# F of all chunks loaded four tokens a partition, its gate sums by 32-row tiles, and a new order

## The chip, the cores and the metric

The kernel runs on one core of a Trainium2 chip. The metric is the device time of one execution, in microseconds. Three runs of the kernel before took 181.86, 181.94 and 181.51 us, median 181.86.

## The reference

A gated linear attention (4 batches, 8 heads, 768 tokens, 48 columns a head) feeds a two-layer network without biases:

```python
f = 1.0 / (1.0 + np.exp(-f_logit))
for t in range(S):
    state = f[:, :, t, :, None] * state + np.einsum('bhd,bhe->bhde', k[:, :, t], v[:, :, t])
    y[:, :, t] = np.einsum('bhd,bhde->bhe', q[:, :, t], state)
x = y as [3072 tokens, 384]
h = x @ w_in                    # 384 x 2048
out = np.maximum(0.01 * h, h) @ w_out   # 2048 x 384
```

## The kernel before

**Tiling.** The 768 tokens are cut into 6 chunks of 128. A unit `u` is one chunk of one batch: 24 units, units 0 to 3 being the first chunk. For a unit, with `g` the running sum of log(1 + exp(-f_logit)) inside the chunk, K is scaled by exp(g) (`em`) and Q by exp(-g) (`a`); both are turned so that the head's columns lie on partitions; scores are their product, masked to the lower triangle (`mask`); `mix` adds the masked scores times V and Q times the state of the batch; `state` adds K times V to the state, which is then multiplied by the decay of the whole chunk (`a_end`). The 128 x 384 result `xn` of a unit is turned (`x`) and goes through the network: `up` makes 256 of the 2048 columns of `h` for a pair of units `m` (6 products of 256 columns), `up_act` takes them out of PSUM through the leaky ReLU, `down` makes one half (8 products of 384 columns) of a unit's output, and `put` and `out_dma` bring it out.

**The gate sums.** For units 4 to 23, `load_part(u, "f", ...)` loads F of one unit with a token on each partition, so every run of bytes is 48 numbers, 192 bytes, as it is for K, Q and V. ACT takes exp (`gate_exp`, L307) and ln (`gate_ln`, L310); `gate_pe` makes the running sums with one product against the triangle `ut` (L316) and the sums of the whole chunk with four one-column products (L319), all in one bank of PSUM; `decay_em` (L323), `decay_a` (L326) and a small exp (L328) take them out.

**The first chunk** has functions of its own, named `q_...`. Its F, K and Q are loaded four tokens a partition (runs of 768 bytes): batch `b` lies on every fourth partition from `b`. `q_gate_pe(hh, pp, bk)` makes the sums of one pair of heads for all four batches with four products of 512 columns (L226), `q_decay_act` (L230) takes them into `emT` and `aT` (which lie in the buffers `gT4` and `gT3`), `q_turn_pe` turns K and Q, and `q_mul` (L247) multiplies them on DVE, 256 columns at a time. `idle_pe` (L144) puts products of zeros into PE's queue where PE would otherwise stand still.

**The order.** One long list of calls, written out at the end of the kernel, gives every engine its order: each engine takes its instructions in the order of the list and waits for what they need. PSUM has eight banks, and every call names the bank that it uses. All loads of K, Q, V and F, the transposes by DMA and the stores go through SP's queue (at the start also ACT's); the weights W_in and W_out go through POOL's queue, cast to bf16 on the way (`load_w_in(0)` and `(1)` are the two halves of W_in). Outputs are stored from a pool of four buffers.

## Time and profile before

| | |
|---|---|
| runs | 181.51, 181.86, 181.94 us |
| span of the profiled execution | 181.4 us |
| what lies around the span | 0.5 us, taken as the median of the runs less the span |
| PE (matmul) busy | 172.7 us, 95% |
| weight loads, PE | 136.6 us, 75% |
| ACT busy | 121.5 us, 67% |
| DVE busy | 87.0 us, 48% |
| POOL busy | 55.7 us, 31% |
| DMA packets | 115014, of them 107440 under 512 bytes |
| read from HBM | 25.17 MB, written 4.72 MB |

The profile tells of one execution. PE is its matmul engine, PEld its weight loads, DVE the vector engine, ACT the scalar engine, POOL the GpSimd, SP the queue of most DMAs; a q behind a name (SPq) is an engine's sequencer. A busy PE is a bound from above, since the ends of its matmuls are modelled. A row of groups gives line, engine, operation, output and inputs, how often, the busy time, the mean of one in nanoseconds, and the idle time just before it with what ended it. The chain gives start, length and piece, in order of time.

### The profile page before, as it was taken

Reading aid. Unit: us, or ns where it says so; the run is one execution under the profiler, and the core shown is the slowest. Engines: PE = TensorE matmul, PEld = TensorE weight load, DVE = VectorE, ACT = ScalarE, POOL = GpSimd, SP = SyncE. Lnnn points to the kernel's source line nnn. Section 1 sums busy time; section 2 is a strip of 40 time slices with the busy share of each in tenths; the row PEclk is TensorE's granted clock in tenths of the full one; section 3 lists DMA queues with packets and bytes.
Section 4 is the critical chain, followed back from the end, with each engine's and each line's share of the span. In section 5 each row is a group of like instructions: output and inputs, shape, how many; then the busy total and the mean of one; then the engine's idle time right before and its main releaser. Section 6 shows DMA issues by size and latency. Waiting matters only on the chain.

```text
span 181.4 us, 4739 instructions
## 1 busy us (share of the span) xinstructions
PE 172.7 (95%) x1850; PEld 136.6 (75%) x1850; DVE 87.0 (48%) x193; ACT 121.5 (67%) x259; POOL 55.7 (31%) x109
## 2 busy tenths in 40 slices
PE   4999999999999999899999999999999999999993
PEld 2567799768679697697778677797786696796972
DVE  7449970253748538438465355374372370430000
ACT  2595789577979696496776777686763494471831
POOL 8092463122256532223415208313252220000000
PEclk9999999999999999999999999999999999999999
DMA  4999989989999999998999999999999796211202
GB/s 149 294 199 188 212 161 212 210 169 205 224 182 249 166 196 182 192 196 177 223 208 186 217 163 219 213 196 196 144 221 199 143 276 140 91 22 25 87 0 89
DMA packets 115014, 31.83 MB, mean 175 GB/s; under 512 B 107440, under 2 KB 113712, under 8 KB 114992
## 3 DMA queue, kind: packets, MB, share of 16 engines
q1 hardware_dynamic: 113072, 27.99, 80.8%
q0 software_dynamic: 1376, 3.15, 9.5%
q10 hardware_dynamic: 544, 0.39, 0.7%
q8 instruction: 14, 0.23, 0.6%
q14 instruction: 8, 0.07, 0.1%
HBM read 25.17 MB, written 4.72 MB: 165 GB/s over the span
## 4 chain that ended last, share of the span: by engine, by line
PE 61%; DMA 15%; SPq 12%; ACT 5%; issue 3%; DVE 1%; POOL 1%; ACTq 0%; POOLq 0%
PE ps L451 23%; PE ps L431 21%; DMA v_raw<-in_v_dram 6%; DMA f_raw<-in_f_logit_dram 6%; SPq L171 6%; SPq L347 5%; DMA fq<-in_f_logit_dram 3%; PE ps L226 2%; PE ps L442 2%; ACT gT L436 2%; PE ps L456 1%; PE ps L144 1%; SPq L475 1%; PE ps L390 1%; PE ps L398 1%
## 5 line engine op out<-in xcount | busy, mean ns | idle before, releaser
L451 PE MATMUL ps<-w_out_b,gT 128*128 128x384 bf16 x368 | 65.5, 326 | 0.0
L431 PE MATMUL ps<-xT,w_in 128*128 128x256 bf16 x528 | 64.4, 273 | 0.2 <-ACT gT L436 0.2
L436 ACT ACTIVATE gT<-ps 128x512 bf16<-128x512 f32 x88 | 51.4, 603 | 9.6 <-PE ps L431 7.7
L431 PEld LDWEIGHTS <-w_in 128*128 128x128 bf16 x528 | 55.9, 114 | 2.2 <-issue 0.4
L451 PEld LDWEIGHTS <-gT 128*128 128x128 bf16 x368 | 34.6, 98 | 19.8
L380 DVE TENSOR_TENSOR wm<-ps,ut 128x512 bf16<-128x512 f32 x40 | 25.2, 683 | 13.4 <-PE ps L369 12.6
L150 ACT COPY osb<-ps 128x384 f32<-128x384 f32 (+1 forms) x23 | 10.7, 465 | 17.8 <-PE ps L451 14.8
L300 POOL CAST sb<-sf 64x192 bf16<-64x192 f32 x40 | 14.3, 358 | 17.4 <-PE ps L387 11.6
L307 ACT ACTIVATE f_raw<-f_raw 128x384 f32<-128x384 f32 x20 | 10.6, 529 | 10.5 <-DMA f_raw<-in_f_logit_dram 10.3
L152 DVE CAST v_b<-v_raw 128x384 bf16<-128x384 f32 x15 | 7.9, 528 | 15.6 <-DMA v_raw<-in_v_dram 15.6
L335 POOL TENSOR_TENSOR kqh<-q_raw,a_t 128x384 bf16<-128x384 f32 x9 | 8.5, 945 | 20.4 <-ACT a_t L326 9.0
L331 POOL TENSOR_TENSOR kqh<-k_raw,em_t 128x384 bf16<-128x384 f32 x8 | 7.3, 916 | 22.7 <-ACT em_t L323 12.6
L323 ACT ACTIVATE em_t<-ps 128x384 bf16<-128x384 f32 x20 | 9.9, 494 | 4.8 <-PE ps L316 3.6
L331 DVE TENSOR_TENSOR kqh<-k_raw,em_t 128x384 bf16<-128x384 f32 x12 | 6.7, 556 | 10.4 <-ACT em_t L323 10.1
L412 POOL TENSOR_TENSOR sf<-sf,a_end 128x192 f32<-128x192 f32 x16 | 8.9, 556 | 7.1 <-DVE sf L407 6.7
L335 DVE TENSOR_TENSOR kqh<-q_raw,a_t 128x384 bf16<-128x384 f32 x11 | 7.5, 684 | 6.9 <-ACT a_t L326 6.7
L310 ACT ACTIVATE lf<-f_raw 128x384 bf16<-128x384 f32 x20 | 10.5, 527 | 0.3
L152 POOL CAST v_b<-v_raw 128x384 bf16<-128x384 f32 x9 | 4.7, 533 | 17.2 <-DMA v_raw<-in_v_dram 17.2
L326 ACT ACTIVATE a_t<-ps 128x384 bf16<-128x384 f32 x20 | 9.9, 495 | 0.0
L144 PE MATMUL ps<-fill 128*128 128x256 bf16 x47 | 8.5, 347 | 1.1 <-DVE uq L128 1.1
L406 DVE TENSOR_TENSOR sf<-sf,ps 64x192 f32<-64x192 f32 x16 | 5.5, 341 | 6.3 <-issue 3.5
L398 PE MATMUL ps<-v_b,kqh 128*128 128x96 bf16 x80 | 6.7, 206 | 1.2 <-DVE v_b L152 1.0
(88 smaller groups left out, 194.5 us busy)
## 6 DMA issues: line engine op xcount, KB each, us to landing
v_raw<-in_v_dram SPq DMA_DIRECT2D x24, 192.0 KB, 4.1
out_dram<-osb SPq DMA_DIRECT2D x23, 192.0 KB, 3.1
f_raw<-in_f_logit_dram SPq DMA_DIRECT2D x20, 192.0 KB, 4.0
k_raw<-in_k_dram SPq DMA_DIRECT2D x20, 192.0 KB, 4.3
q_raw<-in_q_dram SPq DMA_DIRECT2D x20, 192.0 KB, 4.2
w_in<-in_moe_w_in_dram POOLq DMA_DIRECT2D x2, 768.0 KB, 10.1
w_out_b<-in_moe_w_out_dram POOLq DMA_DIRECT2D x4, 384.0 KB, 7.1
kq<-in_k_dram SPq DMA_DIRECT2D x4, 192.0 KB, 4.5
```

Of the source, the lines that this page charges most:

```text
L150: eng.copy(out=out, in_=in_)
L152: eng.tensor_copy(out=out, in_=in_)
L171: nc.sync.dma_start(out=t, in_=src[b, :, c * C:(c + 1) * C, :].rearrange("h t d -> t h d"))
L300: nc.gpsimd.tensor_copy(out=state_b[b][r, :, e * D:(e + 1) * D], in_=state_f[b][r])
L307: nc.scalar.activation(raw[u]["f"], raw[u]["f"], AF.Exp, scale=-1.0)
L310: nc.scalar.activation(lfs[u % R_LF][:, :, 0:D], raw[u]["f"], AF.Ln, bias=1.0)
L331: eng.tensor_mul(khs[u % R_KQS][:, :, 0:D], raw[u]["k"], em_ts[u % R_EM])
L335: eng.tensor_mul(qhs[u % R_KQS][:, :, 0:D], r["q"], a_ts[u % R_EM])
L380: nc.vector.tensor_mul(wms[e][u % R_WM], bank(bk).rearrange("p (i n) -> p i n", i=P2), ut[:, None, :].to_broadcast([128, P2, 128]))
L431: nc.tensor.matmul(bank(bk)[:, i * 256:(i + 1) * 256], w_in_p[ff // 8][:, kk, ff // 4 % 2, :, ff % 4], xTs[m % R_XT][:, kk].rearrange("p a ...
L436: nc.scalar.activation(gTs[m % GBUFS][:, 2 * g:2 * g + 2].rearrange("p f a n -> p (f a n)"), bank(bk), AF.Prelu, alpha=0.01)
L451: nc.tensor.matmul(bank(bk)[:, 0:KD], g_part(u)[:, ff, :], w_out_b[:, ff, :], start=(ff == 0), stop=(ff == NF - 1))
```

## The change

- **F of chunks 1 to 5** is now loaded as that of the first chunk: `load_f(c, b)` puts the 128 tokens of batch `b` on the 32 partitions from 32 b, four tokens a partition (runs of 768 bytes). The four batches of a chunk fill one buffer: `fq` for even chunks, `kq` (after K of the first chunk) for odd ones. Exp and ln run for a whole chunk in two halves of 768 columns.
- **The running sums** of a chunk take 16 products (`gate_pe`, L330): for each of the four tokens a partition, one product for each batch, on the 32 partitions of that batch alone, into that batch's own bank. The matrix against which they run, `upto`, is made once by `upto_pe` and `put_upto`. The sums of the whole chunk take 16 products of four columns (`end_pe`) and one small exp (`end_act`), in place of four products and one small exp for each unit.
- **The first chunk:** the 32 partitions from 32 b hold batch `b` for F, K and Q, in place of every fourth partition. F comes in half loads (four heads), four on SP and four on ACT. The gate sums are made for a pair of batches and two pairs of heads in one bank; DVE's products `q_mul` take 512 columns.
- Outputs are stored from eight buffers, four of which lie in `qq`. The rings of raw loads have 7 buffers in place of 6.
- **The list of calls is new** as a whole.

Core of the diff:

```diff
-    R_RAW, R_KQS, R_LF, R_EM, R_AEND, R_V, R_KQT, R_WM, R_XN, R_XT = 6, 4, 3, 3, 8, 6, 4, 4, 4, 4
+    R_RAW, R_KQS, R_EM, R_V, R_KQT, R_WM, R_XN, R_XT = 7, 4, 8, 6, 4, 4, 4, 4
...
-        eng.dma_start(out=t[b::4, h, :, :].rearrange("p h j d -> p h (j d)"),
+        eng.dma_start(out=t[32 * b:32 * b + 32, h, :, :].rearrange("p h j d -> p h (j d)"),
...
-    first_load(nc.scalar, "f", 2)
-    first_load(nc.sync, "f", 0)
-    first_load(nc.sync, "f", 1)
-    first_load(nc.scalar, "f", 3)
...
+    for hh in range(2):
+        for b in range(B):
+            first_load((nc.sync, nc.scalar)[b // 2], "f", b, hh)
...
-    def q_gate_pe(hh, pp, bk):
-        for i in range(4):
-            nc.tensor.matmul(bank(bk), lfq[hh][:, i, 2 * pp:2 * pp + 2, :],
-                             steps[:, i].rearrange("p b t j -> p (b t j)"), start=(i == 0), stop=(i == 3))
+    def q_gate_pe(hh, bp, bk):
+        for pp in range(2):
+            for i in range(4):
+                nc.tensor.matmul(bank(bk)[:, 256 * pp:256 * pp + 256], lfq[hh][:, i, 2 * pp:2 * pp + 2, :],
+                                 steps[:, i, 2 * bp:2 * bp + 2].rearrange("p b j t -> p (b j t)"), start=(i == 0), stop=(i == 3))
...
+    def q_mul(dst, by, hh, bp, bk):
+        nc.vector.tensor_mul(dst[hh][:, bp].rearrange("p a b (t j) -> p (a b) j t", j=4),
+                             bank16(bk)[:, 512 * bp:512 * bp + 512].rearrange("p (m j t) -> p m j t", m=4, j=4),
+                             by[:, bp, 2 * hh:2 * hh + 2, :].rearrange("p a (b j t) -> p (a b) j t", b=2, j=4))
...
-        nc.tensor.matmul(cs[:, 0:H * D], ut, lf[:, :, 0:D], start=True, stop=True)
-        if c < NCH - 1:
-            for p in range(P2):
-                nc.tensor.matmul(cs[:, H * D + p:H * D + p + 1], lf[:, 2 * p:2 * p + 2, :], ones_col,
-                                 start=True, stop=True)
+    def load_f(c, b):
+        nc.sync.dma_start(out=fcs[c % 2][32 * b:32 * b + 32].rearrange("p h j d -> p h (j d)"),
+                          in_=f_logit[b, :, c * C:(c + 1) * C, :].rearrange("h (t j) d -> t h (j d)", j=4))
...
+    def upto_pe(bk):
+        for j in range(4):
+            nc.tensor.matmul(bank(bk)[:, j * 128:(j + 1) * 128], rows[:, j, :], ut, start=True, stop=True)
...
+    def gate_pe(c, *bks):
+        lf = lfc[c % 2]
+        for j in range(4):
+            for b in range(B):
+                r = slice(32 * b, 32 * b + 32)
+                nc.tensor.matmul(bank(bks[b])[:, 0:H * D], upto[r, j, :], lf[r, j, :, 0:D], start=(j == 0), stop=(j == 3))
+
+    def end_pe(c, bk):
+        for p in range(P2):
+            for j in range(4):
+                nc.tensor.matmul(bank(bk)[:, p * B:(p + 1) * B], lfc[c % 2][:, j, 2 * p:2 * p + 2, :], own,
+                                 start=(j == 0), stop=(j == 3))
...
     q_exp_act(0)
     q_ln_act(0)
-    load_part(0, "v", v)
     q_exp_act(1)
-    idle_pe(24, 7)
-    q_gate_pe(0, 1, 0)
+    idle_pe(24, 0)
+    idle_pe(19, 1)
+    q_gate_pe(0, 1, 2)
...
```

ACT at the start, first as it stood before, then as it stands now (`gT4` is `emT`, `gT3` is `aT`, `ps0` to `ps7` are the banks):

```order
L69 DMA fq_74<-in_f_logit_dram 32x8x192 x2
L82 ACT_TABLE_LOAD
L219 ACTIVATE fq_74<-fq_74 128x768
L222 ACTIVATE lfq0_117<-fq_74 128x16x48
L219 ACTIVATE fq_74<-fq_74 128x768
L222 ACTIVATE lfq1_118<-fq_74 128x16x48
L230 ACTIVATE gT4_236<-ps0_64 128x512
L230 ACTIVATE gT3_235<-ps0_64 128x512
L230 ACTIVATE gT3_235<-ps1_65 128x512
```

In the changed kernel ACT starts so:

```order
L76 ACT_TABLE_LOAD
L68 DMA fq_71<-in_f_logit_dram 32x4x192 x4
L212 ACTIVATE fq_71<-fq_71 128x768
...
L224 ACTIVATE gT4_237<-ps3_64 128x512
L224 ACTIVATE gT4_237<-ps4_65 128x512
L224 ACTIVATE gT4_237<-ps5_66 128x512
L224 ACTIVATE gT4_237<-ps2_63 128x512
L224 ACTIVATE gT3_236<-ps4_65 128x512
L145 CAST qhq0_121<-qq_73 128x16x48
L224 ACTIVATE gT3_236<-ps3_64 128x512
L224 ACTIVATE gT3_236<-ps5_66 128x512
L224 ACTIVATE gT3_236<-ps2_63 128x512
```

The table load moved ahead of the loads, the four decays of K stand ahead of those of Q, and one half of the cast of Q came to ACT, among the decays.

POOL at the end of its preparations, before and now:

```order
L183 COPY seen_237<-kq_75 128x1
L152 CAST khq0_119<-kq_75 128x16x48
L187 DMA w_in0_112<-in_moe_w_in_dram 128x3x1024
L187 DMA w_in1_113<-in_moe_w_in_dram 128x3x1024
L152 CAST qhq0_121<-qq_76 128x16x48
L152 CAST v_b0_206<-v_raw0_186 128x384
L152 CAST v_b1_207<-v_raw1_187 128x384
L268 TENSOR_TENSOR wm10_220<-wm10_220,ut_95 128x512
```

In the changed kernel the same place of POOL reads:

```order
L147 CAST qhq1_122<-qq_73 128x16x48
L180 DMA w_in1_113<-in_moe_w_in_dram 128x3x1024
L147 CAST v_b0_203<-v_raw0_178 128x384
L147 CAST v_b1_204<-v_raw1_179 128x384
L261 TENSOR_TENSOR wm10_217<-wm10_217,ut_96 128x512
L180 DMA w_in0_112<-in_moe_w_in_dram 128x3x1024
L261 TENSOR_TENSOR wm11_218<-wm11_218,ut_96 128x512
```

The two halves of W_in moved behind the cast of Q, the second of them also behind a mask of scores; the cast of K went to DVE.

PE at the first gate sums after the first chunk (unit 4 before, chunk 1 now):

```order
L316 LDWEIGHTS ut_95
L316 MATMUL ps7_71<-lf1_130,ut_95 128x384
L319 LDWEIGHTS lf1_130
L319 MATMUL ps7_71<-ones_col_110,lf1_130 128x1
...
L431 LDWEIGHTS w_in1_113
```

In the changed kernel PE has there, with each weight load after the first left out:

```order
L330 LDWEIGHTS upto_128
L330 MATMUL ps6_67<-lfc1_118,upto_128 128x384
...
L330 MATMUL ps1_62<-lfc1_118,upto_128 128x384
...
L330 MATMUL ps3_64<-lfc1_118,upto_128 128x384
...
L330 MATMUL ps5_66<-lfc1_118,upto_128 128x384
```

One product and four small ones into one bank became four rounds of these four products, into four banks in turn.

More of the change, by code (lines that the diff above doesn't have):

```diff
@@ new lines @@
+    turn_pe(4, 2)
+    down(3, 0, 6)
+    decay_em(7, 5)
+    decay_a(6, 3)
+    k_scale(V, 7)
+    turn_q(A, 4, 2)
+    put(A, 1, 7)
+    turn_k(V, 4, 2)
+    score1_pe(4, 5, 3)
+    load_f(2, 2)
+    k_scale(V, 6)
+    q_state_pool(2)
+    load_part(5, 'v', v)
+    decay_em(5, 1)
+    decay_a(5, 1)
+    q_scale(G, 6)
+    cast_v(A, 4)
+    end_pe(1, 7)
+    load_part(5, 'q', q)
+    mask(4, 0, 5)
+    end_act(1, 7)
+    put(A, 2, 4)
+    turn_pe(7, 2)
+    mask(4, 1, 3)
+    turn_q(A, 7, 2)
+    load_f(3, 2)
@@ new lines @@
+    x_pe(8, 2)
+    decay_a(12, 0)
+    down(6, 1, 3)
+    x_out(A, 8, 2)
+    mask(11, 1, 5)
+    decay_a(15, 7)
+    up(4, 3, 4)
+    load_f(4, 3)
+    mask(11, 0, 6)
+    out_dma(0)
+    mask(10, 1, 1)
+    cast_v(V, 10)
+    put(V, 6, 3)
+    up(4, 5, 2)
+    mix_pe(11, 5)
+    mix_pe(10, 6)
+    y_out(A, 10, 6)
+    load_part(15, 'v', v)
+    up(4, 4, 1)
+    y_out(A, 11, 5)
+    decay_em(12, 0)
+    up(4, 7, 3)
+    up(4, 6, 6)
+    decay_em(15, 7)
+    x_pe(10, 5)
+    x_pe(11, 0)
+    x_out(V, 11, 0)
@@ L1290 @@
+    out_dma(19)
+    up_act(11, 6, 7)
+    up(11, 3, 6)
+    up(11, 4, 3)
+    up_act(11, 3, 6)
+    up_act(11, 5, 1)
+    up_act(11, 4, 3)
+    up(11, 0, 7)
+    up_act(11, 0, 7)
+    down(20, 1, 5)
+    out_dma(18)
+    up_act(11, 2, 4)
+    put(A, 21, 0)
+    up_act(11, 7, 2)
+    down(22, 0, 6)
+    down(22, 1, 6)
+    out_dma(17)
+    down_cols(23, 192, 1)
+    put(V, 22, 6)
     out_dma(21)
[L1291 to L1294 removed]
+    out_dma(22)
+    put(V, 20, 5)
```

1650 lines of the change are left out of this document (771 added, 879 removed).

## Prediction

> **What bounds the kernel now.** I read the page first, then busy time by stretch, the groups inside the middle stretch, the chain of work that ended last, and the waits. The page's span, and two stretches (columns: length; busy us and count of PE, PEld, DVE, ACT, POOL; granted clock; DMA share; GB/s):
>
> ```profile
> span 181.4 us, 4739 instructions
> ```
>
> ```profile
> 21.20:54.00 32.80, 32.80 (x368) 26.44 (x366) 15.01 (x35) 25.43 (x55) 11.87 (x23) 1.00 0.99 195
> 54.00:132.00 78.00, 75.63 (x877) 61.68 (x875) 43.54 (x89) 58.00 (x133) 27.25 (x50) 1.00 1.12 196
> ```
>
> PE is the bound almost everywhere. From 21.2 on its visible idle time is 78.00 - 75.63 = 2.4 us, all of it in the second stretch, where the DMA share is 1.12. PE's ends are modelled, so I count that stretch as well: the largest and the smallest of its ten PE groups, and what one matmul costs in an unbroken run of the chain.
>
> ```profile
> L431 PE MATMUL ps<-xT,w_in 128*128 128x256 bf16 x275 | 34.2, 273 | 0.2 <-ACT gT L436 0.2
> L451 PE MATMUL ps<-w_out_b,gT 128*128 128x384 bf16 x156 | 28.6, 326 | 0.0
> ...
> L319 PE MATMUL ps<-ones_col,lf 128*128 128x1 bf16 x48 | 2.9, 164 | 0.0
> ```
>
> ```profile
> 34.70 0.45 PE ps L344 x8
> ...
> 81.71 0.55 PE ps L369 x16
> ...
> 141.07 0.16 PE ps L316
> ...
> 162.74 5.20 PE ps L451 x32
> 167.94 5.24 PE ps L431 x48
> ```
>
> A product of `up` costs 5.24/48 = 0.109 us, one of `down` 5.20/32 = 0.1625. So 275 x 0.109 + 156 x 0.1625 = 55.3, and the other eight groups by their own runs in the chain 18.1, together 73.4 us of work in 78. The waits are therefore between 2.4 us (visible) and 4.6 us (counted). What is late is mostly a load:
>
> ```profile
> POOL v_b L152 <- DMA v_raw<-in_v_dram: 17.2, 7, 5.7
> DVE v_b L152 <- DMA v_raw<-in_v_dram: 15.6, 14, 2.7
> ```
>
> The rest that isn't work is the start: the chain is 21.34 us old when the first `up` stands on it.
>
> ```profile
> 6.64 0.85 ACT fq L219
> 7.52 0.85 ACT lfq L222
> 8.41 1.90 PE ps L226 x8
> ...
> 13.83 1.42 PE ps L144 x13
> ...
> 21.34 2.62 PE ps L431 x24
> 23.96 0.23 PE ps L278 x8
> 24.20 0.17 PE ps L398 x4
> ```
>
> **The change, part by part.** The sum is made against the span, 181.4 us; the median of the runs, 181.86, is 0.46 above it.
>
> *The start until the first gate sum.* Before, 24 fill products stood ahead of it, behind a wait on `uq` (they share bank 7); now 43 stand there, on banks 0 and 1, with no such wait.
>
> ```profile
> 1.59 0.29 PE L124 MATMUL ps<-rep 128*128 128x128 bf16 x1 [1.59 <-POOL rep L93]
> 2.94 5.28 PE L144 MATMUL ps<-fill 128*128 128x256 bf16 x24 [1.06 <-DVE uq L128]
> ```
>
> They start at about 1.7. The 24 took 0.22 us each; later ones 1.42/13 = 0.109. With 24 slow and 19 fast that is 1.7 + 5.28 + 2.07 = 9.05, against 8.41 before. If the slow rate lasts until 8.4 by time rather than by count, 31 are slow and it is 9.8; if it ends by 5 us, 8.1. The half loads of F may land earlier, but the table load (1.28 us in before, then behind two loads) is now ahead of ACT's four; either way the fills cover it, so this earns nothing.
>
> *From there to the first `up`.* Three rows set the path, with the page's group rows for one instruction:
>
> ```profile
> L230 ACT ACTIVATE gT<-ps 128x512 f32<-128x512 f32 x8 | 4.0, 616 | 0.0
> L247 DVE TENSOR_TENSOR kTq<-ps,gT 128x256 bf16<-128x256 bf16 x8 | 3.0, 414 | 0.2 <-ACT gT L230 0.2
> L272 DVE TENSOR_TENSOR wm<-ps,ut 128x512 bf16<-128x512 f32 x6 | 3.8, 683 | 0.0
> ```
>
> The two gate sums end at 9.05 + 16 x 0.109 + 0.2 = 11.0. ACT then does four decays of K, one of Q, a cast of Q (0.85, as its other ops on 768 elements) and two more decays: 7 x 0.62 + 0.85 = 5.2, to 16.2. DVE's 512-column products have no row; the nearest, a mask of that size, gives 0.62 to 0.68, twice a 256-column one 0.83: I take 0.65. Eight then cost 5.2 instead of 16 x 0.414 = 6.6, but only the last three follow the late decays: 18.1. Six masks and a cast of V (at most another 7 x 0.62) reach 22.4, and the order puts `mix` and `state` of unit 3 (0.23 + 0.17, as in the chain at 23.96) ahead of the first `up`: 22.8, against 21.2. The same 0.4 us was done after the first `up` before, so the start costs +1.2 net; by the ends of the first step, +0.2 to +2.0.
>
> The order also puts the first half of W_in behind POOL's cast of Q, which waits for Q's landing, and past the cast of V; before, both halves went out ahead of it:
>
> ```profile
> 10.15 1.72 POOL L187 DMA_DIRECT2D w_in<-in_moe_w_in_dram x2
> 11.66 0.58 DVE L152 CAST qhq<-qq 128x768 bf16<-128x768 f32 x1 [2.27 <-DMA qq<-in_q_dram]
> 11.87 1.06 POOL L152 CAST qhq<-qq 128x768 bf16<-128x768 f32 x1
> DMA to landing us min/median/max: 8.3/10.1/11.9
> ```
>
> It goes out at 11.66 + 1.06 = 12.7 and lands at 21.0 to 24.6, median 22.8: just in time, 0 to +2 us. POOL's masks and V casts queue behind its 0.86 us, off the path. The second half follows a POOL mask at about 18.6 and lands at 26.9 to 30.5; its first reader is the eighth `up`, at 22.8 + 7 x 0.655 + 0.8 = 28.2. I take nothing for either.
>
> *The gate sums of the other five chunks.* Before, 4 x 0.16 = 0.64 us a chunk, and four one-column products a unit; now 16 products of 384 columns on 32 rows each, four neighbours on different rows and banks. No row shows 32 rows. One after the other they cost 16 x 0.163 = 2.6, four at once 0.65. The nearest row is that of 64 rows: 16 of 128 columns in 0.55 where full ones would take 2 x 0.45 = 0.90 (L344), 1.63 times of a possible 2. The same share of 4 is 3.27: 0.80, so +0.16 a chunk, +0.8 in all; ends 0 and +9.8. The column sums keep their count, 16 a chunk. The four products for `upto` add 0.2. The Trainium skill (TensorE: Matmul & The Clock Gate, Part 3) says that four row tiles of 32 rows run at once and measured 3.07 times; by it a chunk would cost 0.85 and the sum would be 0.25 us higher. The 64-row group agrees in kind; no row here shows 32 rows.
>
> The four sums hold four banks, and ACT needs 8 decays = 4.0 us to free them:
>
> ```profile
> L307 ACT ACTIVATE f_raw<-f_raw 128x384 f32<-128x384 f32 x20 | 10.6, 529 | 10.5 <-DMA f_raw<-in_f_logit_dram 10.3
> ...
> L323 ACT ACTIVATE em_t<-ps 128x384 bf16<-128x384 f32 x20 | 9.9, 494 | 4.8 <-PE ps L316 3.6 <-PE ps L319 0.8 <-issue 0.2
> ```
>
> Behind the sums of chunk 1, three halves of `down` (3 x 1.3) stand on PE, which need no ACT, so I cost it at nothing. Without that cover, a chunk would lose up to 4 us.
>
> *Exp and ln of F, the loads.* ACT has 40 instructions of 0.53 (L307 and its Ln) less and 20 of 0.85 more: 21.2 - 17.0 = 4.2 us less, and 12 small ones fewer. ACT is busy for 25.4 + 58.0 of the two stretches' 110.8 us, so this counts only through the waits. F's 20 loads keep their size but move runs of 768 bytes in place of 192. The two kinds of load side by side:
>
> ```profile
> 3.00:5.00 2.00, 2.00 (x10) 1.40 (x10) 2.00 (x8) 0.42 (x1) 1.68 (x5) 1.00 1.03 341
> 100.00:110.00 10.00, 9.55 (x100) 7.45 (x99) 4.23 (x10) 7.88 (x19) 2.70 (x5) 1.00 1.27 187
> ```
>
> The first window holds loads of the first chunk (768 bytes), the second mostly 192. A load of 196.6 KB takes 1.05 us of all queues at 187 GB/s and 0.58 at 341: 0.47 us a unit less, of 4.2 for a unit's four, where the DMA share was over 1. That can take all of the 2.4 to 4.6 us of waits, or nothing, if the new order puts its own in their place: POOL has 13 scalings of Q instead of 9, and all transposes, loads and stores still share SP's queue. I take -1.6, a third of the upper bound, because the new order gives V's loads other places in the queue too.
>
> **The sum:** +1.2 + 0.8 + 0.2 - 1.6 = +0.6: span 182.0, time 182.5 us. The tail, one DMA after the last columns, stays.
>
> **The rivals.**
> - *The loads were the whole trouble (faster).* All 4.6 us go and nothing takes their place: +1.2 + 1.0 - 4.6 = -2.4, time 179.5. For it: the waits above name loads, and every stretch of idle PE lies where the DMA share is over 1. Against: 21 to 54 has a share of 0.99 and no idle PE. It decides from 2.2 us of waits removed.
> - *New waits of the new order (slower).* Half of the new gate sums lose half of their cover, 5 x 0.5 x 2 = 5 us more: 187.5. It decides from 1 us on, as the forecast's gain from the waits is 1.6. For it: chunk 5's sums are followed by `up`, which needs ACT too. Against: banks alternate there with `down` between.
> - *Loads onto neighbouring partitions are slower (slower).* K and Q of the first chunk (8 x 0.197 MB, 4.6 us at 341 GB/s) now each fill 32 neighbours instead of every fourth partition. If that costs between nothing and half of the rate, Q lands 0 to 4.6 us later, 2.3 in the middle, and so does W_in's first half: 182.5 + 2.3 = 184.8. No row here shows neighbours. The Trainium skill (SBUF — State Buffer, Door 1: The DMA port swizzle) says that partitions 0 to 31 reach only 8 of 16 ports; by it the delay would be an estimated 2.6 us.
> - *The 32-row products run one after the other (the change doesn't do what it says).* +9.8 in place of +0.8: 191.5. Against: the 64-row row.
>
> **How the numbers follow.** Forecast 0.38 (182.5, its own range 181 to 184), faster rival 0.31, new waits 0.15, neighbours 0.10, one after the other 0.06. The range 178.6 to 187.8 leaves out the last and the outer ends. A difference of under 0.3% (181.3 to 182.4) can't be told from no change. Faster: the rival's 0.31 and 0.07 of the forecast's lower end, 0.38; within: 0.13 of the forecast's middle; slower: the other 0.18 of it and the last three, 0.49.
>
> **What would show it.** The first `up` at 22 to 23.5 with the first gate sum at 8.1 to 9.8; the gate group (32*128, 128x384) in runs of about 0.8 us for 16 in the chain; f loads landing in under 4.0 us; PE idle between 54 and 132 under 2.4 us; no new releaser of PE over 1 us. The prediction is wrong if PE waits for W_in or Q at the start, if 16 gate products take over 1.5 us, or if the waits of the middle stretch don't change.

## The result, and the profile after

The changed kernel takes 189.4 us (188.4 to 189.9) where the kernel before, on the same chip, takes 181.9: the ratio is 1.038, 95% interval 1.031 to 1.045. The forecast was 182.5 with a range to 187.8.

The page of the changed kernel: span, busy time, PE's clock in 40 slices, DMA packets, SP's queue.

```profile
span 186.5 us, 4848 instructions
...
PE 175.3 (94%) x1951; PEld 140.8 (75%) x1951; DVE 90.4 (48%) x182; ACT 111.9 (60%) x223; POOL 60.2 (32%) x118
...
PEclk9999889999999999999999999999999999999998
...
q1 hardware_dynamic: 97744, 27.99, 82.6%
```

PE is still busy for 94%, so the busy line doesn't tell what went wrong. SP's queue has 15,300 packets fewer than before and a larger share of a longer span. The chain shows the place:

```profile
1.69 6.12 PE ps L139 x43
7.80 3.51 PE ps L220 x32
...
11.96 2.46 DVE kTq L239 x2
...
16.52 4.79 DVE qTq L239 x4
...
21.36 0.91 PE ps L254 x16
...
26.65 0.81 PE ps L448 x6
...
43.48 0.76 PE ps L330 x16
```

The first `up` (L448 now) stands at 26.65, against 21.34 before (21.18 in the timeline of PE, from which the table below takes its numbers). That is 5.3 us, and the two spans differ by 5.1: between these two profiles, nothing is lost or won behind the first `up` (159.85 against 160.06). In front of it stand DVE's products of 512 columns, four of Q in 4.79 us with nothing between them. The groups of the first 26.6 us, with masks of the same size beside them:

```profile
L239 DVE TENSOR_TENSOR qTq<-ps,gT 128x512 bf16<-128x512 bf16 x4 | 4.8, 1356 | 0.0
L239 DVE TENSOR_TENSOR kTq<-ps,gT 128x512 bf16<-128x512 bf16 x4 | 4.8, 1343 | 0.7 <-ACT gT L224 0.7
L265 DVE TENSOR_TENSOR wm<-ps,ut 128x512 bf16<-128x512 f32 x6 | 3.8, 693 | 0.0
```

One product takes 1.35 us, or 4.79/4 = 1.2 from start to start, where the forecast had 0.65. Q also came later: the first cast of it, now ACT's, waits for the landing until 13.98 (11.66 before, on DVE).

```profile
13.98 0.83 ACT L145 CAST qhq<-qq 128x768 bf16<-128x768 f32 x1 [1.07 <-DMA qq<-in_q_dram]
```

The middle stretch, in the form of the forecast's windows, has 2.07 us of visible idle PE, where it had 2.37:

```profile
54.00:132.00 78.00, 75.93 (x951) 62.12 (x949) 42.58 (x88) 56.41 (x115) 32.43 (x59) 1.00 1.11 190
```

A profile is one execution. That of the kernel before was longer than most: its span is 181.4, while the other executions of this kernel take about 1.75 to 1.85 us more than their span (not the 0.5 us put down above), so a median of 181.9 means a span of about 180.1. That of the changed kernel is the fastest of its four. So the profiles differ by 5.1 us, the medians by 7.5 and the means, which the ratio compares, by 6.9; if the first `up` stood where it did in the profiles, which can't be seen for the other executions, some 2 us were lost behind it. What follows counts in ratios, in which one hundredth is 1.82 us. The ratios leave out executions clearly slower than the fastest of the same kernel (among them five of twelve for loads onto every fourth partition without strides, and the profiled one of the changed kernel with fewer fills), so they are given in place of medians.

| run | ratio to the kernel before (95%) | first `up`, us |
|---|---|---|
| kernel before | 1 | 21.2 |
| changed kernel | 1.0379 (1.0311 to 1.0446) | 26.65 |
| DVE writes in order | 1.0307 (1.0221 to 1.0393) | 24.83 |
| DVE without strides | 1.0253 (1.0190 to 1.0316) | 22.35 |
| first loads alternate | 1.0401 (1.0338 to 1.0464) | 27.13 |
| every fourth partition | 1.0326 (1.0279 to 1.0374) | 26.61 |
| every fourth, no strides | 1.0112 (1.0071 to 1.0153) | 22.84 |
| same, less 12 loads of F | 1.0002 (0.9979 to 1.0025) | 22.85 |
| before, less 12 loads of F | 0.9897 (0.9860 to 0.9934) | 20.95 |
| before, F in whole rows | 0.9820 (0.9776 to 0.9864) | 20.95 |
| before, neighbours | 1.0073 (1.0032 to 1.0114) | 22.95 |

### The profile page after: what moved, and what is told of

It is laid out like the page before. It is cut to its first block, busy times and chain, and to the rows that moved or that the text cites. A ratio compares the mean times of both kernels' runs of the same rounds, so it can differ in the third digit from the quotient of the medians.

```text
span 186.5 us, 4848 instructions
## 1 busy us (share of the span) xinstructions
PE 175.3 (94%) x1951; PEld 140.8 (75%) x1951; DVE 90.4 (48%) x182; ACT 111.9 (60%) x223; POOL 60.2 (32%) x118
## 4 chain that ended last, share of the span: by engine, by line
PE 73%; DVE 8%; DMA 7%; SPq 4%; issue 2%; ACT 2%; POOL 1%; POOLq 0%; DVEq 0%; ACTq 0%
PE ps L468 26%; PE ps L448 25%; PE ps L139 4%; DMA v_raw<-in_v_dram 3%; PE ps L459 3%; DVE qTq L239 3%; DMA kq<-in_f_logit_dram 2%; SPq L364 2%; PE ps L220 2%; DMA k_raw<-in_k_dram 2%; PE ps L415 2%; PE ps L386 1%; PE ps L407 1%; PE ps L473 1%; DVE kTq L239 1%
## 5 line engine op out<-in xcount | busy, mean ns | idle before, releaser
L468 PE MATMUL ps<-w_out_b,gT 128*128 128x384 bf16 x368 | 64.3, 326 | 0.0
L448 PE MATMUL ps<-xT,w_in 128*128 128x256 bf16 x528 | 63.2, 273 | 0.2
L453 ACT ACTIVATE gT<-ps 128x512 bf16<-128x512 f32 x88 | 48.6, 623 | 23.7 <-PE ps L448 23.3
L448 PEld LDWEIGHTS <-w_in 128*128 128x128 bf16 x528 | 56.1, 114 | 1.7 <-issue 0.5
L468 PEld LDWEIGHTS <-gT 128*128 128x128 bf16 x368 | 34.8, 98 | 21.2 <-issue 0.3
L397 DVE TENSOR_TENSOR wm<-ps,ut 128x512 bf16<-128x512 f32 x40 | 25.4, 684 | 21.2 <-ACT gT L453 15.0
L352 POOL TENSOR_TENSOR kqh<-q_raw,a_t 128x384 bf16<-128x384 f32 x13 | 12.9, 997 | 40.8 <-ACT gT L453 13.4
L348 DVE TENSOR_TENSOR kqh<-k_raw,em_t 128x384 bf16<-128x384 f32 x12 | 9.2, 776 | 15.3 <-ACT em_t L342 13.5
L147 DVE CAST xn<-ps 128x384 bf16<-128x384 f32 x14 | 7.7, 555 | 11.8 <-PE ps L407 7.8
L145 ACT CAST xn<-ps 128x384 bf16<-128x384 f32 x10 | 4.6, 479 | 12.9 <-PE ps L407 11.0
L147 DVE COPY qq<-ps 128x384 f32<-128x384 f32 x7 | 3.8, 553 | 16.9 <-issue 14.7
L139 PE MATMUL ps<-fill 128*128 128x256 bf16 x68 | 10.8, 317 | 0.7 <-DVE qTq L239 0.7
L139 PEld LDWEIGHTS <-fill 128*128 128x128 bf16 x68 | 7.5, 114 | 1.6
L407 PE MATMUL ps<-v_b,wm 128*128 128x48 bf16 x160 | 7.4, 183 | 0.9 <-DVE v_b L147 0.9
```

The source lines that it names most:

```text
L139: nc.tensor.matmul(bank(bk)[:, 0:256], fill[:, 0:128], fill[:, 0:256], start=True, stop=True)
L147: eng.tensor_copy(out=out, in_=in_)
L348: eng.tensor_mul(khs[u % R_KQS][:, :, 0:D], raw[u]["k"], em_ts[u % R_EM])
L352: eng.tensor_mul(qhs[u % R_KQS][:, :, 0:D], r["q"], a_ts[u % R_EM])
L397: nc.vector.tensor_mul(wms[e][u % R_WM], bank(bk).rearrange("p (i n) -> p i n", i=P2), ut[:, None, :].to_broadcast([128, P2, 128]))
L448: nc.tensor.matmul(bank(bk)[:, i * 256:(i + 1) * 256], w_in_p[ff // 8][:, kk, ff // 4 % 2, :, ff % 4], xTs[m % R_XT][:, kk].rearrange("p a ...
```

## Experiments: DVE's products

**Writes in order.** The products write as the result lies and read with strides.

```diff
-        nc.vector.tensor_mul(dst[hh][:, bp].rearrange("p a b (t j) -> p (a b) j t", j=4),
-                             bank16(bk)[:, 512 * bp:512 * bp + 512].rearrange("p (m j t) -> p m j t", m=4, j=4),
-                             by[:, bp, 2 * hh:2 * hh + 2, :].rearrange("p a (b j t) -> p (a b) j t", b=2, j=4))
+        nc.vector.tensor_mul(dst[hh][:, bp].rearrange("p a b (t j) -> p (a b) t j", j=4),
+                             bank16(bk)[:, 512 * bp:512 * bp + 512].rearrange("p (m j t) -> p m t j", m=4, j=4),
+                             by[:, bp, 2 * hh:2 * hh + 2, :].rearrange("p a (b j t) -> p (a b) t j", b=2, j=4))
```

> The eight 512-column products of DVE write kTq and qTq in the order in which they lie there; both inputs are read with strides instead. Same result. Changed kernel now: 1.34 us busy each and 1.19 from start to start (four in 4.77). Theory A, the scattered write is what costs: 0.65 to 0.85 each (twice the 256-column product of the kernel before is 0.83), first `up` some 3 us earlier, at about 23.5, time 189.4 - 3 = about 186.4. Rival B, any 512-column product of these operands costs 1.2 whatever the order: 1.2 to 1.35 each, time unchanged within 0.5 us. Rival C, a strided read costs as much as a strided write: 1.2 or more, time unchanged or longer.

**Without strides.** All three operands run as they lie.

```diff
+        nc.vector.tensor_mul(dst[hh][:, bp].rearrange("p a b n -> p (a b n)"),
+                             bank16(bk)[:, 512 * bp:512 * bp + 512],
+                             by[:, bp, 2 * hh:2 * hh + 2, :].rearrange("p a n -> p (a n)"))
```

> The eight products read and write everything as it lies, with no strides; the tokens of kTq and qTq then stand in another order, so the masked scores of the first chunk and what follows from them are not the reference's, while the work is the same. Theory A (write): 0.62 to 0.70 each, like a mask of 512 columns (0.62 to 0.68), first `up` at 22.5 to 23.5, time 185.5 to 186.5. Rival B (size and operands): 1.2 each, time unchanged. Rival C (any stride): 0.62 to 0.70 here and over 1.2 in the run with ordered writes.

The groups of the start, first of the run that writes in order, then of the one without strides:

```profile
L239 DVE TENSOR_TENSOR kTq<-ps,gT 128x512 bf16<-128x512 bf16 x4 | 3.9, 1044 | 1.4 <-ACT gT L224 1.4
L239 DVE TENSOR_TENSOR qTq<-ps,gT 128x512 bf16<-128x512 bf16 x4 | 3.9, 1030 | 0.0
```

```profile
L239 DVE TENSOR_TENSOR qTq<-ps,gT 128x512 bf16<-128x512 bf16 x4 | 2.6, 686 | 0.0
L239 DVE TENSOR_TENSOR kTq<-ps,gT 128x512 bf16<-128x512 bf16 x4 | 2.5, 683 | 1.9 <-ACT gT L224 1.9
```

Without strides a product takes what a mask of its size takes, 0.68 us; strided reads make it 1.04, a strided write 1.35. So the size isn't the cause (rival B falls); theory A was right on the write and wrong on the reads, for which rival C has a part. A strided operand also has more dimensions in its pattern; the two weren't tried apart. The first `up` comes to 22.35 without strides, 0.45 from the forecast's 22.8. But of the 4.3 us won at the start only 2.3 arrive in the time (1.0379 to 1.0253; 187.0 us by the median, where 185.5 to 186.5 was expected), as waits behind it grow. That for V was 1.1 in the changed kernel, that for W_out is new:

```profile
PE ps L415 <- ACT v_b L145: 1.9, 1, 1.9
PE ps L468 <- DMA w_out_b<-in_moe_w_out_dram: 1.4, 2, 0.8
```

Both are loads: an engine that comes earlier finds V and W_out not there yet.

Not all of the 4.3 us is DVE's. The last group of scores (L254, 16 products behind the last Q product) starts at 21.36 in the changed kernel and at 17.77 without strides: 3.6 us. The other 0.7 lies behind it, where PE's clock was at half: between 21.3 and 24.9 us its mean is 0.53. The run with F by tokens, described below, has the same start and a full clock there (1.00 between 21.5 and 25.0):

```profile
22.68 0.62 PE L254 MATMUL ps<-qTq,kTq 64*128 64x128 bf16 x16 [0.88 <-DVE qTq L239]
...
26.93 0.81 PE L448 MATMUL ps<-xT,w_in 128*128 128x256 bf16 x6
```

From these scores to the first `up` it takes 4.25 us, and the changed kernel 5.29: the slow clock cost 1.0 us at the start of the profiled execution. All four executions of the changed kernel have a mean clock of 0.988 to 0.991, all four without strides 1.00, so the 2.3 us of the ratio hold some of it too.

## Experiments: loads onto neighbouring partitions

**First loads alternate.** F on SP and ACT in turn, K and Q in the batch order 0, 2, 1, 3.

```diff
-            first_load((nc.sync, nc.scalar)[b // 2], "f", b, hh)
+            first_load((nc.sync, nc.scalar)[b % 2], "f", b, hh)
...
-        for b in range(B):
+        for b in (0, 2, 1, 3):
             first_load(nc.sync, name, b)
```

> The loads of the first chunk go out in the batch order 0, 2, 1, 3, F's on SP and ACT in turn, so that loads that follow each other fill partitions of the lower and of the upper half. In the changed kernel Q lands at about 13.9 us, in the one before at 11.66; between 5 and 11 us the DMAs moved 225 to 269 GB/s against 271 to 341. Theory D, neighbouring partitions limit the rate of loads in flight together: Q lands up to 2.2 us earlier, the 5:11 windows go over 270 GB/s, and the time falls by 0 to 2 us (the DVE products stand behind the cast of Q only in part). Rival: the rate is that of 32 partitions whatever is in flight beside them, or comes from the half loads of F: Q at 13.5 to 14, time unchanged. The Trainium skill (SBUF — State Buffer, Door 1: The DMA port swizzle) has partitions 0 to 31 on 8 of 16 ports; by it the alternation should win back most of it.

Q's cast starts at 13.3 in place of 13.98 and the windows between 5 and 11 us have 238 to 251 GB/s: nearly the rival, and no gain. That the alternation should win back most of it was a misreading of the page: the Trainium skill (SBUF — State Buffer, "Can I just issue two DMAs to hit both halves?") says that two DMAs to different halves don't add up. The trace agrees: 238 to 251 GB/s lie inside the 225 to 269 of the loads that don't alternate.

**Every fourth partition**, alone and together with products without strides:

```diff
-        eng.dma_start(out=t[32 * b:32 * b + 32, h, :, :].rearrange("p h j d -> p h (j d)"),
+        eng.dma_start(out=t[b::4, h, :, :].rearrange("p h j d -> p h (j d)"),
...
-        nc.sync.dma_start(out=fcs[c % 2][32 * b:32 * b + 32].rearrange("p h j d -> p h (j d)"),
+        nc.sync.dma_start(out=fcs[c % 2][b::4].rearrange("p h j d -> p h (j d)"),
```

> The changed kernel, its order unchanged; all loads that put four tokens on a partition (F, K, Q of the first chunk, F of the others) fill every fourth partition instead of 32 neighbours. The batches are then mixed up and the output is not the reference's; every instruction is the same. Changed kernel: packets of 768 bytes 52.9 ns on the mean, of 192 bytes 19.7, all packets 174.5 us of 16 queues; the kernel before 38.8, 17.0 and 166.7. Theory D, 32 neighbours take the packets at a lower rate and slow what runs beside them: 768 bytes under 42 ns, 192 bytes about 17, Q lands at 11.7 to 12.5 in place of 13.9, time 189.4 - 1 to 3. Rival H, the packets are slower because of what the order puts side by side: 50 ns and over, Q at 13.4 to 14, time unchanged within 0.7.

> Both: loads onto every fourth partition, and DVE's eight products without strides (0.65 us from start to start). Output not the reference's for both reasons. With the products alone the first `up` went from 26.65 to 22.35 and the median from 189.4 to 186.95: 1.8 us of 4.3 were lost again in waits for V and W_out. Theory D says that these waits come from slow packets: here the first `up` is at 21 to 22, the stretch behind it as long as in the changed kernel (159.9) or shorter, time 182.5 to 184.5. Rival G, the new order in SP's and POOL's queues is what makes the waits: the stretch stays at 162 to 163.5 us and the time at 185.5 to 187.

**Neighbours in the kernel before:** `t[b::4, ...]` becomes `t[32 * b:32 * b + 32, ...]` there, nothing else.

> The kernel before, its order unchanged; F, K and Q of the first chunk go onto 32 neighbouring partitions for each batch in place of every fourth (the batches are then mixed up and the output is not the reference's). It prices the neighbours alone, at the start alone. By the packets of the changed kernel against the one with every fourth partition (768 bytes: 52.9 against 44.6 ns), 3328 packets cost 1.7 us more of all queues: Q and the loads of V behind it land 0.7 to 2 us later and the first `up` stands 0.5 to 2 us later, time + 0.5 to 2. Rival: the order has room there, time unchanged within 0.5 us.

Means over all packets of each trace (count x ns), and all packets together in us of 16 queues:

| kernel | 768 bytes | 192 bytes | all |
|---|---|---|---|
| before | 3328 x 38.8 | 86016 x 17.0 | 166.7 |
| before, neighbours | 3328 x 55.0 | 86016 x 18.4 | 176.5 |
| changed | 8448 x 52.9 | 65536 x 19.7 | 174.5 |
| changed, every fourth | 8448 x 44.6 | 65536 x 17.1 | 157.8 |
| changed, every fourth, no strides | 8448 x 43.0 | 65536 x 16.8 | 154.7 |

The neighbours make a 768-byte packet 19 to 42% longer, and the 192-byte packets beside it 8 to 15%. That is theory D in kind, though not in size: 44.6 ns is over the 42 it had put, and the 5.8 ns that are left to 38.8 come with the new order and F's later loads. In the order of the kernel before, the timeline shows the price: Q's cast at 13.67 in place of 11.66, the first `up` at 22.95 in place of 21.18, the time longer by 0.73% = 1.3 us.

```profile
13.67 0.56 DVE L152 CAST qhq<-qq 128x768 bf16<-128x768 f32 x1 [3.27 <-DMA qq<-in_q_dram]
...
22.95 2.78 PE L431 MATMUL ps<-xT,w_in 128*128 128x256 bf16 x24
```

In the changed kernel the faster loads alone give 1.0 us of time for 17 us of queue time, by ratios whose intervals overlap, and the first `up` doesn't move (26.61): DVE stands on the path there. With DVE out of the way they give 2.6 (1.0253 to 1.0112), all of it behind the first `up` (22.35 and 22.84): 163.3 us stand behind it in the profile with neighbours and 160.5 with every fourth. Theory D had put the first `up` at 21 to 22 and the stretch at 159.9 or less, rival G at 162 or more.

Q comes only 0.7 us earlier for it, at 13.26, and not at 11.7 to 12.5. Its loads go out later than in the kernel before, since four half loads of F, where two loads stood, and K's are ahead of them in SP's queue. In the timeline of SP, with every fourth partition and no strides, they start at 7.00, in the kernel before at 5.05:

```profile
7.00 2.58 SPq L68 DMA_DIRECT2D qq<-in_q_dram  x4
```

So a part of Q's delay isn't the neighbours': with every fourth partition 1.6 us of it stay. (Onto neighbours Q's loads go out at 5.78, but take 5.8 us to land.)

The windows of the middle stretch, of every fourth alone:

```profile
54.00:132.00 78.00, 76.30 (x961) 62.68 (x962) 43.69 (x89) 56.11 (x115) 31.71 (x57) 1.00 0.97 182
```

The DMA share fell from 1.11 to 0.97 and PE's visible idle time only from 2.07 to 1.70.

**F by tokens:** the changed kernel with F's later loads in runs of 192 bytes on all partitions.

```diff
+        nc.sync.dma_start(out=fcs[c % 2][:, :, b, :],
+                          in_=f_logit[b, :, c * C:(c + 1) * C, :].rearrange("h t d -> t h d"))
```

> The changed kernel; the 20 loads of F for chunks 1 to 5 take runs of 192 bytes onto all 128 partitions, as in the kernel before, into the same buffers (a batch then lies in another place, so the gate sums mix tokens and the output is not the reference's). Everything else, the first chunk's loads too, stays. It asks what the new form of these loads is worth in the new order. Theory D (32 neighbours take packets slowly and slow what is beside them): the 20480 packets of 192 bytes cost 20 x 1.09 = 22 us of all queues in place of the 20 x 0.85 = 17 that 256 x 52.9 ns give, but the other 192-byte packets fall from 19.7 to about 17 ns (65536 x 2.7 / 16 = 11 us): all packets 174.5 + 5 - 11 = about 168, time within 1 us of 189.4. Rival (run length is what counts): 180 us of packets, time 190 to 192.

Packets 169.5, as theory D had it; but the time is 190.8 by the median, as the rival had it, the ratio 1.0473 (1.0424 to 1.0523). So the new form of F's loads seems worth some 1.7 us in the new order, even on neighbours, although the queues are busy for longer with it; the two intervals overlap a little. Why less queue time went with more time here stays open.

**One head of all batches a load**, onto all 128 partitions, which still computes the reference; and the same with Q's products without strides:

```diff
+                nc.sync.dma_start(out=fcs[c % 2][:, h].rearrange("p j d -> p (j d)"),
+                                  in_=f_logit[:, h, c * C:(c + 1) * C, :].rearrange("b (t j) d -> b t (j d)", j=4))
```

> The changed kernel with the reference's result: every four-token load takes one head of all four batches onto all 128 partitions (128 runs of 768 bytes), in place of one batch onto 32 neighbours. F of a chunk then takes 8 issues on SP instead of 4, K and Q of the first chunk 8 each. Theory D: packets of 768 bytes at 40 to 45 ns, of 192 bytes at about 17, as with every fourth partition, and the time falls as there, to 188 to 189; Q lands no later than 13.3 if the 8 more issues of 0.3 to 0.4 us on SP fit beside the transfers. Rival I, SP's queue is the limit: 20 + 8 more issues take 9 us of SP, loads stand later, time over 190.

> The run before this one and, with the reference's result too, Q's products of the first chunk without strides: qTq keeps the token order in which PE leaves it, the mask of the first chunk has its columns in that order, and the stores of units 0 to 3 put the rows back; K's products write in order as in the first of these runs (0.97 us apart). Expected: the four Q products at 0.65, K's at 0.97, first `up` at 23 to 23.5, time 185 to 186 if Theory D holds for loads over all partitions, 186.5 to 187.5 if only the products gain.

A miss: 223.7 us (ratio 1.229) and 232.0 (1.261). The packets are fast, 39 ns, but the DMA rows of the first run's page show another limit in the first slices of 5.6 us:

```profile
DMA  1222479978579596699677999945997949603033
GB/s 42 93 93 93 122 147 204 207 148 161 134 152 180 135 166 149 157 194 173 158 155 173 211 142 160 159 112 137 181 257 161 163 87 172 192 3 88 23 142 106
```

93 GB/s at a share of two tenths (0.27 between 5.6 and 22.2 us), with loads queued: about a quarter of the queues worked. The Trainium skill (DMA: Bandwidth & Descriptors, "Why a DMA increments its semaphore by 16 and not by 1") says that a DMA uses the largest number of engines up to 16 that divides the slowest dimension of both its patterns; these are 4 (batches) and 128, so 4 engines. The share of 0.27 agrees with 4 of 16. The experiment therefore says nothing on rival I.

**Q in its own order**, loads as in the changed kernel, which still computes the reference:

```diff
+        if dst is qTq:
+            nc.vector.tensor_mul(dst[hh][:, bp].rearrange("p a b n -> p (a b n)"),
+                                 bank16(bk)[:, 512 * bp:512 * bp + 512],
+                                 by[:, bp, 2 * hh:2 * hh + 2, :].rearrange("p a n -> p (a n)"))
...
+            for j in range(4):
+                nc.sync.dma_start(out=to[j::4, :], in_=osb[32 * j:32 * j + 32])
```

> The changed kernel, its loads as they are, with the reference's result: Q's products of the first chunk run without strides (qTq keeps the token order in which PE leaves it; the mask of the first chunk has its columns in that order; the stores of units 0 to 3 go out in four parts of 32 rows that put the order right, 12 more issues on SP), K's write in order with strided reads. Q products at 0.65 from start to start, K's at 0.97, first `up` at 23 to 23.8, between the run with ordered writes (24.83; 188.4) and the one without strides (22.35; 186.95): 187 to 188. If the 12 issues stand in the way of loads: 188 to 189.5.

Q's products took 0.68 busy each and the first `up` came at 22.93, 3.7 earlier than in the changed kernel; yet the time was 190.0 (1.0447, 1.0409 to 1.0486): no gain, and over the 189.5 that was put for the bad case. PE waits for V for 1.5 and 1.1 us, and for longest on the transposes in SP's queue, for which the changed kernel has no wait:

```profile
PE ps L394 <- DMA kqT<-kqh: 2.2, 1, 2.2
```

The 12 more issues stand in that queue ahead of them; that they are its cause wasn't tried apart.

## Experiments: the gate products

**Batch by batch**, and **all on the same rows**:

```diff
-        for j in range(4):
-            for b in range(B):
+        for b in range(B):
+            for j in range(4):
```

```diff
-                r = slice(32 * b, 32 * b + 32)
+                r = slice(0, 32)
```

> The 16 products of 32 rows of each chunk's gate sums go batch by batch: four on the same rows and the same bank follow each other, where neighbours were on different rows and banks. Same result. In the changed kernel 16 take 0.76 us in the chain. Theory E, neighbours on different rows run at once: here 16 x 0.163 = 2.6 us, 5 chunks x 1.85 = +9 us at most, less what the waits of the middle stretch take up (2 us): 189.4 + 7 to 9. Rival, a 32-row product of 384 columns is short by itself: 0.8 us again and the time unchanged.

> The changed kernel; all 16 products of a chunk's gate sums read the 32 rows of batch 0, so no two can lie on different rows. The sums of batches 1 to 3 are then those of batch 0. In the changed kernel 16 take 0.76 us in the chain, batch by batch 0.79. Theory E, PE overlaps products on different rows however they are queued: here 16 x 0.163 = 2.6 us, PE busy in that group 80 x 0.163 = 13 us. Rival, a product of 32 rows is short by itself: 0.8 us again.

The chain, batch by batch and then on the same rows:

```profile
43.72 0.79 PE ps L330 x16
```

```profile
43.95 2.70 PE ps L330 x16
```

In another order 16 products take 0.79 (ratio 1.0371, unchanged); on the same rows 2.70, and the time of the one execution is 203.5. So the overlap of different rows is real, 3.4 times, and doesn't need neighbours in the queue: products queued four in a row for the same rows still overlapped with those of other rows behind them. My first expectation, 7 to 9 us more, was wrong there.

## Experiments: what F's loads are worth, and what is left

**Whole rows in the kernel before**, and **12 loads of F left out** in both:

```diff
+            nc.sync.dma_start(out=t.rearrange("p h d -> p (h d)"),
+                              in_=flat[c * C * H * D:(c + 1) * C * H * D].rearrange("(p n) -> p n", p=C))
```

```diff
     def load_f(c, b):
+        if c > 2:
+            return
```

> The kernel before, its order unchanged; each of the 20 loads of F for units 4 to 23 takes 128 runs of 1536 bytes that lie one behind the other in place of 1024 runs of 192 bytes, onto the same 128 partitions. The tokens of F are then others, so the output is not the reference's; the size and the number of loads are the same. Packets of 192 bytes took 17.0 ns each in the profile before, packets of 1536 bytes (stores) 74: a load falls from 1.09 us of all queues to 0.59, 20 of them by 10 us. Theory F, the waits of the middle stretch come from how long the loads occupy the queues: visible idle of PE in 54:132 falls from 2.4 to under 1.2 us and the time by 1.0 to 2.4 us. Rival G, they come from where the loads stand in SP's queue: idle and time unchanged within 0.5 us.

> The kernel with loads onto every fourth partition and products without strides (185.6 us), less the 12 loads of F for chunks 3 to 5: their exp and ln run on what the buffers hold. It asks what is left of the loads' part. Theory G, the waits left are those of loads in the queues: with 12 x 0.85 = 10 us of all queues gone, the time falls by 1 to 2 us, to 183.5 to 184.5. Rival J, what is left against the kernel before is work and order on PE (the start 1.5 us later, gate sums and `upto` about 1 us): time within 0.5 us of 185.6.

> The kernel before less the 12 loads of F for chunks 3 to 5 (exp and ln run on what the buffers hold), as the run of the changed kernel without them (182.46). With F's loads out of the way in both, the difference is that of the start and of PE's work. Theory J, these differ by the start's 1.5 us and about 1.0 of gate sums and `upto`: the kernel before less F takes 179.5 to 180.2. Rival G, the new order of SP's queue costs as well: below 179, and then the difference is over 3.5 us. Rival K, the waits for loads alone part the two kernels: within 1 us of 182.5.

With whole rows the kernel before takes 179.4 us (0.982), and PE's visible idle in the middle stretch is gone:

```profile
54.00:132.00 78.00, 78.00 (x927) 64.64 (x925) 44.84 (x93) 60.66 (x139) 31.14 (x55) 1.00 1.10 205
```

So the waits of the middle do come from how long loads occupy the queues (theory F, over its upper end: 3.3 us against 2.4). Leaving 12 loads out takes 2.0 us from the changed kernel (1.0112 to 1.0002) and 1.9 from the one before (1 to 0.9897). F's loads weigh the same in both orders, and what parts the two stays 1.9 us. The timelines of PE, first of the changed kernel so reduced, then of the kernel before:

```profile
22.85 0.82 PE L450 MATMUL ps<-xT,w_in 128*128 128x256 bf16 x6
```

```profile
20.95 2.78 PE L432 MATMUL ps<-xT,w_in 128*128 128x256 bf16 x24
```

With spans of 180.9 and 178.9, 158.05 and 157.95 us stand behind the first `up`. With these loads out, all of the difference is the start (theory J, without its 1.0 of gate sums).

**Fewer fills:** `idle_pe(19, 1)`, the second group of fills, is taken out of three kernels: every fourth without strides, the changed kernel, and the one that writes in order.

> The kernel with loads onto every fourth partition and products without strides, less the second group of 19 fill products ahead of the first gate sum. There the first gate sum stood at 9.04 us though its input was ready at 7.02, and the first decay of K (10.99) came after K (10.09). Theory L, the fills are what is left of the later start: the gate sums start at about 7.1, the first `up` 1 to 1.9 us earlier than 22.84, time 182.5 to 183.6 in place of 184.6. Rival M, the wait moves to Q's landing (13.1) or PE runs the gate sums at its slow rate: first `up` within 0.5 us of 22.84, time within 0.5 of 184.6.

> The changed kernel less the same 19 fill products, with the reference's result. Its first gate sum stood at 7.64, its K products waited 0.7 us for the decays, and its Q products follow the K products with no gap. Theory L: K products start up to 0.7 us earlier, the time falls by 0 to 0.7. Rival M: the fills also set PE's clock; without them 32 gate products at the slow rate take 7 us in place of 3.5 and the time rises by 1 to 3 us.

> The kernel whose DVE products write in order (ratio 1.0307), less the same 19 fills, with the reference's result. K's products waited 1.4 us there for the decays behind fills. Theory L: 0.5 to 1.4 us less, ratio 1.023 to 1.028. Rival M as above: ratio over 1.033.

The first ended at 1.0130 (1.0063 to 1.0197) against 1.0112: no gain (rival M in the time), but by another mechanism than it named. The gate sums did start earlier, and W_in's first half took the place:

```profile
6.84 3.71 PE L220 MATMUL ps<-steps,lfc 128*128 128x256 bf16 x32 [0.72 <-ACT lfc L215]
...
23.10 0.84 PE L448 MATMUL ps<-xT,w_in 128*128 128x256 bf16 x6 [1.41 <-DMA w_in<-in_moe_w_in_dram]
```

Without that wait the first `up` would stand at 21.7. W_in is issued behind POOL's cast of Q, so by this run's numbers the start can't be earlier than Q's landing (13.1), that cast (0.82) and W_in's 9.2 to 9.8 us to its landing: an estimate of 23.1. The other two: 1.0428 (1.0363 to 1.0493), no gain on the changed kernel (the intervals overlap, so rival M stays unclear there). Its second 16 gate products wait for ACT's Ln until 9.22, and DVE's first product starts at 11.81 in place of 11.96. And 1.0283 (1.0219 to 1.0348), the best version of the changed kernel that computes the reference, some 0.4 us better than with all fills by ratios that overlap. No version that computes the reference beats the kernel before.

## Why the prediction was wrong

Counted from the ratios, the 6.9 us are 2.3 for the strides of DVE's products (with some of the slow clock in it), 2.6 for loads onto neighbours once these are gone, and 2.0 that are left; in the other sequence the first two would be 3.9 and 1.0, as each hides part of the other. By the widths of the intervals the first two are good to some 1.5 us either way, an estimate; the runs without F's later loads put the last at 1.9, all of it at the start.

- **The first gate sum** was put at 9.05 and came at 7.64 (8.39 and 9.04 in runs with the same 43 fills), outside the range of 8.1 to 9.8 in the profile shown. The half loads of F earned nothing, as forecast, and they sent Q out later, which the forecast didn't count. When the fills end does matter: with F by tokens the gate sums start 1.34 later than in the changed kernel and the last scores 1.32 later.
- **DVE's 512-column products: the step that failed.** It took 0.65 us for each, "the nearest, a mask of that size". The row was near in size, not in how the write lies: with the result four bf16 apart one takes 1.2 from start to start. Eight cost 9.6 and not 5.2, and Q's four lie on the path whole, where the forecast had its path run over ACT's decays. (The row set aside, 0.83, stood for strided reads; in that form one takes 0.97.) Where the products take 0.65, the rest of the start held step by step. In the run with every fourth partition and no strides, the first gate sum is at 9.04 (forecast 9.05), the first decay at 10.99 (11.0), the last decay ends at 16.5 (16.2), the last product at 18.4 (18.1), and the first `up` is at 22.84 (22.8). The slow clock behind the scores, 1.0 us, was in no step.
- **W_in** cost nothing, as forecast: no wait for it with the first `up` at 26.65, nor at 22.35 and 22.84. With fewer fills, where it would be at 21.7, it costs 1.4.
- **Gate sums:** 0.76 us for 16 against 0.80; the rival that they run one after the other is out. The cover of the decays by `down` held: in the chain `down` follows the 16 products at 43.48 with no gap. The rival of new waits gets nothing: PE's longest waits behind the first `up` are for V (1.1 and 0.9 us), none for the decays.
- **The loads, -1.6:** a load of F was to take 0.47 us less of all queues. By packets it takes 1024 x 17.0/16 = 1.09 before and 256 x 52.9/16 = 0.85 now, 0.24 less, and slows the others: all packets together rose from 166.7 to 174.5. F's loads landed in 4.7 us, not under 4.0, and visible idle of PE fell by 0.3, from 2.37 to 2.07, not by 1.6. With every fourth partition and no strides it is still 2.11, and 2.0 us are left against the kernel before where the forecast had 0.6: most of the 1.6 didn't come there either. The mechanism was there: put back in the new order, the old form costs 1.7 us more; on all partitions, in the order before, wide runs gain 3.3, to 179.4. That this is nearly the number of the rival in which the loads were the whole trouble (179.5) is luck, as that sum holds 2.2 us for a start and gate sums that this run doesn't have. The 0.47 us rests on 341 GB/s from a window whose loads went to every fourth partition.
- **Neighbours,** a rival with a chance of 0.10 and 2.3 us: right in mechanism: 2.0 us for Q's landing and 1.3 in the time in the order before. In the new order they cost Q 0.7, and most of their price comes later, from F's loads and those beside them, which the rival left out.

So a rival came true together with a product priced too low and a gain from the loads that didn't come, which no case of the forecast had.

## What to carry to other kernels

The price of a vector operation is read from a row with the same layout of all operands, the output first of all: take a row of equal size only if the strides agree, or put a bound of twice that on it. Where a layout is changed so that a later engine gets neighbours, ask what the DMAs and the engine that permutes now pay for it. When two delays end at the same place, undo both, since each alone shows little.

## What was not expected of the hardware

- A tensor product on DVE of 512 columns, PSUM bf16 by SBUF f32 into bf16: 0.68 us without strides, 1.04 with both inputs strided, 1.35 with the write 4 elements apart. The Trainium skill (SBUF — State Buffer, Door 1: The DMA port swizzle) puts how far one can stride for free at 8 bf16 elements; this write, at 4, doesn't agree.
- Loads onto every fourth partition and onto 32 neighbours: 38.8 against 55.0 ns for a packet of 768 bytes, with everything else equal.
- PE's clock, in the page of the kernel with 16 products on the same 32 rows: four of the five groups (at 43.95, 64.36, 84.75 and 139.48 in its chain; not that at 114.80) are followed by a dip. A slice is 5.0 us; the first dip is that of the start.

```profile
PEclk9999799996999699969999999999699999999998
```

That kernel lost 14 us, of which the products themselves explain 5 x 1.94 = 9.7. The changed kernel shows a dip too, near 22 us. Leaving out the two runs of one head a load, whose dips lie elsewhere, six of the seven profiles with the strided write have it, and none of the seven with faster products has one there. The price of that one dip is the 1.0 us above, from one pair of profiles. That the wait for the products brings it on wasn't shown: F by tokens waits as long and has none.
